# An mLSTM cell with expert routing: output gates as exp(-o) inside the divisor of the output

## The chip, the cores and the metric

The kernel runs on one core of one Trainium2 chip. The metric is device time in microseconds (us) for one execution, and the median of several runs is given. One core has TensorE (PE, matrix multiplication, with PEld for its weight loads), VectorE (DVE), ScalarE (ACT), GpSimd (POOL) and SyncE (SP), which here only issues DMA transfers. The engines run side by side and wait for each other through semaphores.

## The reference

Two parts follow each other. The first is a recurrence over 768 time steps for 4 batches and 8 heads of dimension 40:

```python
for t in range(S):
    m_new = np.maximum(f_gate[:, :, t] + m, i_gate[:, :, t])
    f_stab = np.exp(f_gate[:, :, t] + m - m_new)
    i_stab = np.exp(i_gate[:, :, t] - m_new)
    m = m_new
    C = f_stab[..., None, None] * C + i_stab[..., None, None] * einsum('bhd,bhe->bhde', vt, kt)
    n = f_stab[..., None] * n + i_stab[..., None] * kt
    h_tilde = einsum('bhde,bhe->bhd', C, qt)
    nq = einsum('bhd,bhd->bh', n, qt)[:, :, None]
    denom = np.maximum(np.abs(nq), 1.0)
    o = 1.0 / (1.0 + np.exp(-o_gate[:, :, t]))
    y[:, :, t] = o * h_tilde / denom
```

The result, as 3072 rows of 320 numbers, goes to one of eight experts for each row: `relu(x @ w1[e]) @ w2[e]`, with the expert chosen by a hash of the token. Only the last two lines of the loop matter for the change: the output is `h_tilde` times a sigmoid, divided by `denom`.

## The kernel before

The recurrence is done in chunks: 128 time steps of all eight heads of one batch make one **step**, and there are 24 steps (`NT`), 6 (`NB`) for each of 4 batches. A step has attention scores inside the chunk, a state `C` carried from chunk to chunk, and at its end the transposed output `xo` in PSUM, which holds for each head 40 numbers of `h_tilde` and in column `D` the number `nq`. The expert part follows and reads the rows back by gathers.

The output gates `og` are loaded early, in tiles for six steps, and each tile is put through one sigmoid:

```python
groups = [(0, 3)] + [(s, min(s + 6, NT)) for s in range(3, NT, 6)]

def load_o(s):
    for s0, s1 in groups:
        if s == s0:
            tile_o = ld.tile([P, 6, H, D], F32, name="og", bufs=2)
            og[s, "all"] = tile_o[:, : s1 - s0]
            for i in range(s0, s1):
                og[i] = tile_o[:, i - s0]
    nc.sync.dma_start(og[s], rows_of(o_gate, s))

def sigmoid(s):
    o = og[s, "all"]
    nc.scalar.activation(o, o, AF.Sigmoid)                                      # L343
```

The end of a step, and the parts of a step that the working speaks of:

```python
def back(s):                        # xo in PSUM, tag "tr", 4 buffers
    ...
            nc.tensor.transpose(xo[:, hf, i, :], d["hT"][:, hf, i, :], ident[:])    # L424

def finish(s):
    d = st.pop(s)
    hs = d["xo"].rearrange("p f i (x d) -> p f (i x) d", d=DP)
    den = wk.tile([P, 2, PR, 1], F32, name="den")
    nc.vector.tensor_scalar(den[:], hs[:, :, :, D:D1], scalar1=-1.0, scalar2=1.0,
                            op0=ALU.mult, op1=ALU.max)                          # L430
    nc.vector.tensor_tensor(den[:], den[:], hs[:, :, :, D:D1], op=ALU.max)      # L433
    x = wk.tile([P, H, D], F32, name="x")
    xv = x.rearrange("p (j f) d -> p f j d", f=2)
    nc.vector.tensor_tensor(xv, hs[:, :, :, :D], og[s].rearrange(...), op=ALU.mult) # L436
    nc.vector.reciprocal(den[:], den[:])                                        # L439
    eng = nc.vector if s + 1 == NT else nc.gpsimd
    eng.tensor_tensor(xv, xv, den[:].to_broadcast([P, 2, PR, D]), op=ALU.mult)  # L441
    return lambda: nc.sync.dma_start(x_d[s * P : (s + 1) * P, :], ...)          # L442

def pad_q(b, r):                    # writes qp, read by the transposes of turn_q (L288)
    t = qb[b][r] = qps[2 + r % 2]
    nc.vector.tensor_copy(t[:, :, :D], qb[b]["l"][:, :, r * D : (r + 1) * D])   # L280

def entering(s):                    # qs = q times the decay xb, on VectorE (L327)
def state(s):                       # state product on PE (L382); C += it on VectorE (L388)
def weigh(s):                       # w = scores sp times decays w, on VectorE, twice (L359)
```

The order in which one step is written down (each engine keeps this order for its own instructions):

```python
for s in range(NT):
    b, c = s // NB, s % NB
    # ... loads of k, v, q, o and weights
    decayed(s)                      # POOL: C times its decay (L368)
    turn_k(s + 2)                   # PE: transposes of k (L275), ACT copies them
    turn_q(b + 1, ...)              # PE: transposes of q (L288), ACT copies them
    back(s - 1)                     # PE: xo (L424)
    store = finish(s - 1)           # DVE, POOL
    decays(s + 1)                   # PE (L311), ACT: exp (L315)
    if s > 0 and (s, "all") in og:
        sigmoid(s)
    state(s)
    entering(s + 1)                 # PE: xb (L323), DVE: qs
    k_weights(s + 1)                # POOL: kw (L336)
    store()
    scores(s + 1)                   # PE: sp (L351)
    weigh(s + 1)
    pad_q(nb + 1, r)                # for the transpose of q in the next step
    # ... pieces of the routing
    attend(s)                       # PE: ht (L402, L409), ACT: hT (L417)
    if s == 0:
        sigmoid(0)
    # ... more pieces of the routing (tables on PE, L589, from step 13 on)
back(NT - 1)
finish(NT - 1)()
```

In the last steps of the loop some of these calls fall away. q is transposed one batch ahead, so no q is transposed in the last batch (steps 18 to 23). The first step of a batch has no entering state, so steps 5, 11 and 17, which prepare it, have no `entering`. After the loop, TensorE runs a fixed number of matmuls into an unused tile (`spin`, L924) while the first gathers are under way, and then the experts.

Of the kernel before, what the change touches and what calls it, by code (L numbers as in the profile page):

```python
# [8 lines left out]
F32 = mybir.dt.float32  # L9
# [4 lines left out]
AF = mybir.ActivationFunctionType  # L14
ALU = mybir.AluOpType
PSUM = bass.MemoryType.PSUM

P = 128
# [4 lines left out]
def kernel(  # L23
# [24 lines left out]
    nc = tc.nc  # L48
    B, H, S, D = q.shape
# [6 lines left out]
    NT = N // P  # L56
    PR = H // 2
    DP = 64
    D1 = D + 1
# [20 lines left out]
    x_d = nc.dram_tensor("x_rows", (N, Dm), F32, kind="Internal").ap()  # L80
# [24 lines left out]
    def weight_slices(e):  # L105

        W[e], slices = weights(moe_w1[e], moe_w2[e], wpools[e % 3 // 2], w2pools[2 <= e < 6])
        return slices
# [8 lines left out]
    with tc.tile_pool(name="gates", bufs=1) as gp, \  # L117
# [34 lines left out]
        st = {}  # L152
        qb = {}

        def rows_of(t, s):
            b, c = s // NB, s % NB
            return t[b, :, c * P : (c + 1) * P, :].rearrange("h p d -> p h d")

        def load_k(s):
            st[s] = {"k": ks[s % NK], "v": vs[s % NK]}  # L160
            nc.sync.dma_start(ks[s % NK][:, :, :D], rows_of(k, s))

        def load_v(s):
            nc.sync.dma_start(vs[s % NK][:, :, :D], rows_of(v, s))


        groups = [(0, 3)] + [(s, min(s + 6, NT)) for s in range(3, NT, 6)]
        og = {}

        def load_o(s):  # L170
            for s0, s1 in groups:
                if s == s0:
                    tile_o = ld.tile([P, 6, H, D], F32, name="og", bufs=2)
                    og[s, "all"] = tile_o[:, : s1 - s0]
                    for i in range(s0, s1):
                        og[i] = tile_o[:, i - s0]
            nc.sync.dma_start(og[s], rows_of(o_gate, s))

        def load_q(b, part):

            if part == 0:
                qb[b] = {"l": ld.tile([P, H, NB * D], F32, name="ql", bufs=2)}
            hs = slice(part * PR, (part + 1) * PR)
            nc.sync.dma_start(qb[b]["l"][:, hs], q[b, hs].rearrange("h (p r) d -> p h (r d)", r=NB))

        def load_e(b, gs):
            src = ze_d.rearrange("(g b h) i t -> b (h i) g t", g=NC2, h=H)[b]
            nc.scalar.dma_start(
                Ls[b % 2][: 3 * H, :].rearrange("r (g t) -> r g t", t=W2)[:, gs[0] : gs[-1] + 1],
                src[:, gs[0] : gs[-1] + 1],  # L190
            )
# [78 lines left out]
        def turn_k(s):  # L270
            d = st[s]
            d["kT"] = wk.tile([P, PR, P], F32, name="kT")
            tp = ps.tile([P, PR, P], F32, name="tr", tag="tr", bufs=4)
            for j in range(PR):
                nc.tensor.transpose(tp[:, j, :], d["k"][:, 2 * j : 2 * j + 2, :].rearrange("p h d -> p (h d)"), ident[:])  # L275
            nc.scalar.copy(d["kT"][:], tp[:])
# [5 lines left out]
        def turn_q(b, r, cols):  # L282
            if "T" not in qb[b]:
                qb[b]["T"] = wk.tile([P, PR, S], F32, name="qT")
            t = qb[b].pop(r)
            tp = ps.tile([P, PR, P], F32, name="tr", tag="tr", bufs=4)
            for j in range(PR):
                nc.tensor.transpose(tp[:, j, :], t[:, 2 * j : 2 * j + 2, :].rearrange("p h d -> p (h d)"), ident[:])  # L288
            nc.scalar.copy(qb[b]["T"][:, :, cols], tp[:])  # L289


        def load_q0(c):
            t = qb.setdefault(0, {})[c] = qps[c % 2]
            nc.sync.dma_start(t[:, :, :D], rows_of(q, c))

        def turn_q0(c):
            turn_q(0, c, slice(c * P, (c + 1) * P))
# [40 lines left out]
                    kw_T[:, c % 2, c // 2, b * H : (b + 1) * H].unsqueeze(2).to_broadcast([P, H, D]), op=ALU.mult,  # L338
                )

        def sigmoid(s):
            o = og[s, "all"]
            nc.scalar.activation(o, o, AF.Sigmoid)  # L343

        def scores(s):
            d = st[s]
# [14 lines left out]
        def decayed(s):  # L361
            c = s % NB
            if c == 0:
                st["C"] = None
            if c + 1 < NB:
                st["Cn"] = Cs[s % 2]
                if c > 0:
                    nc.gpsimd.tensor_tensor(  # L368
                        st["Cn"][:, :, :D1], st["C"][:, :, :D1], st[s]["dec"][:].to_broadcast([P, PR, D1]), op=ALU.mult,
                    )  # L370
# [48 lines left out]
        def back(s):  # L419
            d = st[s]  # L420
            xo = d["xo"] = ps.tile([P, 2, 2, P], F32, name="xo", tag="tr", bufs=4)
            for hf in range(2):
                for i in range(2):
                    nc.tensor.transpose(xo[:, hf, i, :], d["hT"][:, hf, i, :], ident[:])  # L424

        def finish(s):
            d = st.pop(s)
            hs = d["xo"].rearrange("p f i (x d) -> p f (i x) d", d=DP)
            den = wk.tile([P, 2, PR, 1], F32, name="den")
            nc.vector.tensor_scalar(  # L430
                den[:], hs[:, :, :, D:D1], scalar1=-1.0, scalar2=1.0, op0=ALU.mult, op1=ALU.max,
            )
            nc.vector.tensor_tensor(den[:], den[:], hs[:, :, :, D:D1], op=ALU.max)  # L433
            x = wk.tile([P, H, D], F32, name="x")
            xv = x.rearrange("p (j f) d -> p f j d", f=2)
            nc.vector.tensor_tensor(  # L436
                xv, hs[:, :, :, :D], og[s].rearrange("p (j f) d -> p f j d", f=2), op=ALU.mult,
            )
            nc.vector.reciprocal(den[:], den[:])  # L439
            eng = nc.vector if s + 1 == NT else nc.gpsimd  # L440
            eng.tensor_tensor(xv, xv, den[:].to_broadcast([P, 2, PR, D]), op=ALU.mult)  # L441
            return lambda: nc.sync.dma_start(x_d[s * P : (s + 1) * P, :], x.rearrange("p h d -> p (h d)"))  # L442


        iotas = {}
# [223 lines left out]
        turn_q0(0)  # L669
        load_q0(2)  # L670
        load_o(0)
        load_v(1)
        load_o(1)
# [48 lines left out]
        for s in range(NT):  # L722
            b, c = s // NB, s % NB
            if 0 < s < NT - 3:
                load_k(s + 3)
                if b == 0 and c < 3:
                    load_q0(c + 3)
            if s + 3 < NT:
                load_v(s + 3)
            if c in (2, 4) and b + 2 < B:  # L730
                load_q(b + 2, c // 2 - 1)
            for i in range(2):
                o = s - (s - 3) % 6 + 6 + 2 * ((s - 3) % 6 - 1) + i if s > 2 else 3 + 2 * s + i
                if o < NT and (s < 3 or 1 <= (s - 3) % 6 <= 3):
                    load_o(o)
            if s in (3, 13):
                slices += weight_slices(s // 10)
            if slices:
                slices.pop(0)()
            decayed(s)  # L740
            if s + 2 < NT:
                turn_k(s + 2)
            if b == 0 and c < 4:
                turn_q0(c + 2)
            if b + 1 < B:
                for r in (turns_of if b else first_turns).get(c, ()):
                    turn_q(b + 1, r, slice(r, None, NB))
            if s > 0:
                back(s - 1)
                store = finish(s - 1)  # L750
            if s + 1 < NT:
                decays(s + 1)
            if s == 0:
                load_e(0, [1, 2])
            if c == 3 and b + 1 < B:
                load_e(b + 1, [0, 1, 2])
            if s > 0 and (s, "all") in og:
                sigmoid(s)
            state(s)
            if s + 1 < NT:  # L760
                entering(s + 1)
                if s + 2 < NT:
                    load_a(s + 2, nc.scalar if s == 0 else nc.sync)
                k_weights(s + 1)
            if s > 0:
                store()
            if s + 1 < NT:
                scores(s + 1)
                weigh(s + 1)
            nb = b + (c == NB - 1)  # L770
            if nb + 1 < B and s + 1 < NT:
                for r in (turns_of if nb else first_turns).get((c + 1) % NB, ()):
                    pad_q(nb + 1, r)
            for piece in before.get(s, []):
                piece()
            attend(s)
            if s == 0:
                sigmoid(0)
                gates_turn(g1)
            for piece in after.get(s, []):  # L780
                piece()
        back(NT - 1)
        finish(NT - 1)()

    wpools.append(ctx.enter_context(tc.tile_pool(name="wlate", bufs=1)))
    w2pools.append(ctx.enter_context(tc.tile_pool(name="w2late", bufs=4)))
# [88 lines left out]
    with tc.manual_schedule():  # L875
# [54 lines left out]
        for e in range(E):  # L930
            g, i = e // EG, e % EG
            if e + 2 < E:
                fetch(e + 2)
            h = xp.tile([P, FB, CAP], F32, name="h")
# [23 lines left out]
    with tc.If(nx > 0):  # L958
        with tc.For_i(0, nx, 1) as k:
# [12 lines left out]
            h = xp.tile([P, FB, CAP], F32, name="h")  # L972
# [34 lines left out]
```

## Time and profile before

| What | Value |
|---|---|
| median of 3 runs (lowest to highest) | 426.49 us (426.43 to 426.70) |
| span of the profiled execution | 423.8 us |
| mean granted TensorE clock, share of full speed | 0.988 |
| TensorE busy | 392.1 us, 93% of the span |
| VectorE busy | 136.2 us, 32% |
| ScalarE busy | 134.3 us, 32% |
| GpSimd busy | 117.7 us, 28% |

The profile divides the span into the start of the recurrence (0 to 38 us), its steps (38 to 165 us) and the experts (165 to 424 us). A group row gives the line, the engine, the operation, the tiles and their shapes (partitions x elements), the count, the busy time in us with the mean of one in ns, and after the last bar the idle time of the engine just ahead of these instructions with what ended it. A timeline row gives start and duration in us, the engine, the line and the tiles; in brackets stands the idle time ahead of it and what ended that. Rows that merge several instructions show their count. A busy TensorE isn't TensorE at its peak, because matmuls are pipelined.

### The profile page before, as it was taken

The page shows a single profiled execution, that of the slowest core. Times are in us where ns is not written, and L with a number is a line of the kernel's source. Part 1 is how long each engine was busy: PE and PEld are TensorE (multiplying, and loading weights), DVE is VectorE, ACT ScalarE, POOL GpSimd, SP SyncE. Part 2 cuts the span into 40 slices and gives each one's busy share as a digit, 9 for nine tenths or more (in the row PEclk, how much of TensorE's full clock was granted, in tenths as well). Part 3 has the DMA queues.
Part 4 walks back from the last instruction along what each step waited for, and adds up shares of the span by engine and source line. Part 5 has one row for each costly group of instructions (what it writes and reads, how often), then busy time and mean ns, then how long its engine had stood idle before and what let it go on. Part 6 is the DMA issues. An engine that isn't in the chain of part 4 may idle for free.

```text
span 423.8 us, 7461 instructions
## 1 busy us (share of the span) xinstructions
PE 392.1 (93%) x2892; PEld 262.1 (62%) x2892; DVE 136.2 (32%) x373; ACT 134.3 (32%) x238; POOL 117.7 (28%) x202
## 2 busy tenths in 40 slices
PE   2369999999999997999999999999999999999992
PEld 2247877877887874556657556556556566575551
DVE  7364748776675762220120110210110201201100
ACT  5158786696495471010111111110111101111010
POOL 6364313313433421711402401311302212020021
PEclk9988999999999999999999999999999999999998
DMA  9829998899675630548508217144126100000000
GB/s 173 212 61 177 205 206 188 191 207 223 153 163 126 162 95 33 151 147 254 168 26 263 87 62 224 63 125 160 60 96 185 62 17 29 0 17 30 0 18 30
DMA packets 111784, 51.37 MB, mean 121 GB/s; under 512 B 86624, under 2 KB 105892, under 8 KB 111748
## 3 DMA queue, kind: packets, MB, share of 16 engines
q1 hardware_dynamic: 105898, 39.31, 38.2%
q0 software_dynamic: 2496, 8.20, 6.0%
q10 hardware_dynamic: 3354, 3.37, 2.4%
q8 instruction: 23, 0.38, 0.4%
q14 instruction: 13, 0.11, 0.1%
HBM read 42.00 MB, written 8.63 MB: 119 GB/s over the span
## 4 chain that ended last, share of the span: by engine, by line
PE 84%; ACT 5%; issue 5%; POOL 2%; DVE 1%; ACTq 1%; DMA 1%; POOLq 0%; DVEq 0%
PE mh L836 22%; PE zp L865 21%; PE sp L351 7%; PE ht L409 6%; PE mh L829 6%; PE ht L402 3%; PE mh L924 3%; PE ab L311 2%; PE tr L275 2%; PE xo L424 2%; PE ht L382 2%; PE tr L288 2%; PE tk L589 2%; PE tp L811 1%; PE xb L323 1%
## 5 line engine op out<-in xcount | busy, mean ns | idle before, releaser
L865 PE MATMUL zp<-w2t,h 128*128 128x320 f32 x384 | 105.2, 433 | 0.0
L836 PE MATMUL mh<-xT,w1t 128*128 128x416 f32 x256 | 96.2, 519 | 0.5 <-issue 0.5
L865 PEld LDWEIGHTS zp<-w2t,h 128*128 128x128 f32 x384 | 72.7, 190 | 32.1 <-issue 3.3
L836 PEld LDWEIGHTS mh<-xT,w1t 128*128 128x128 f32 x256 | 46.7, 190 | 42.7 <-issue 41.6
L817 DVE COPY xT<-tp 128x384 f32<-128x384 f32 x16 | 8.9, 558 | 141.4 <-PE tp L813 98.1
L798 POOL DMA_INDIRECT out_dram<-zo,s_idx x26 | 25.7, 988 | 92.5 <-ACT zo L797 92.5
L845 ACT ACTIVATE h<-mh 128x416 f32<-128x416 f32 x32 | 16.6, 517 | 107.4 <-PE mh L829 54.7
L797 ACT COPY zo<-zp 128x320 f32<-128x320 f32 x26 | 11.1, 426 | 101.1 <-PE zp L865 92.9
L843 DVE TENSOR_SCALAR h<-mh 128x416 f32<-128x416 f32 x32 | 18.9, 592 | 52.1 <-PE mh L829 26.3
L359 DVE TENSOR_TENSOR w<-sp,w 128x512 f32<-128x512 f32 x48 | 30.9, 686 | 13.7 <-PE sp L351 10.3
L441 POOL TENSOR_TENSOR x<-x,den 128x320 f32<-128x320 f32 x23 | 16.6, 724 | 61.6 <-DVE den L439 29.6
L351 PE MATMUL sp<-qT,kT 64*128 64x128 f32 x384 | 29.7, 297 | 4.1 <-ACT qT L289 4.1
L351 PEld LDWEIGHTS sp<-qT,kT 64*128 64x128 f32 x384 | 24.9, 199 | 10.7 <-ACT qT L289 5.9
L315 ACT ACTIVATE w<-ab 128x512 f32<-128x512 f32 x48 | 26.8, 614 | 4.6 <-PE ab L311 4.6
L409 PE MATMUL ht<-w,v 128*64 128x128 f32 x384 | 27.1, 285 | 0.0
L791 POOL DMA_INDIRECT xg<-x_rows,g_idx x24 | 23.4, 974 | 12.6 <-issue 12.6
L829 PE MATMUL mh<-xT,w1c 64*128 64x416 f32 x128 | 26.7, 535 | 0.0
L952 POOL COPY hrem<-h 128x256 f32<-128x256 f32 x8 | 3.2, 400 | 81.9 <-ACT h L845 81.9
L417 ACT COPY hT<-ht 128x512 f32<-128x512 f32 x24 | 14.1, 587 | 31.2 <-PE ht L409 31.2
L409 PEld LDWEIGHTS ht<-w,v 128*64 128x64 f32 x384 | 21.2, 140 | 4.0 <-issue 3.1
L289 ACT COPY qT<-tr 128x512 f32<-128x512 f32 x24 | 22.9, 977 | 0.6 <-PE tr L288 0.3
L275 PE MATMUL tr<-ident,k 128*128 128x128 f32 x96 | 17.4, 309 | 4.1 <-POOL R L638 4.1
(181 smaller groups left out, 421.3 us busy)
## 6 DMA issues: line engine op xcount, KB each, us to landing
w2t<-in_moe_w_dram SPq DMA_DIRECT2D x28, 320.0 KB
w1t<-in_moe_w_dram SPq DMA_DIRECT2D x28, 256.0 KB
k<-in_k_dram SPq DMA_DIRECT2D x24, 160.0 KB
v<-in_v_dram SPq DMA_DIRECT2D x24, 160.0 KB
og<-in_o_gate_dram SPq DMA_DIRECT2D x24, 160.0 KB
x_rows<-x SPq DMA_DIRECT2D x24, 160.0 KB
ql<-in_q_dram SPq DMA_DIRECT2D x6, 480.0 KB
w1c<-in_moe_w_dram SPq DMA_DIRECT2D x14, 128.0 KB
```

What stands on the lines that cost most here:

```text
L275: nc.tensor.transpose(tp[:, j, :], d["k"][:, 2 * j : 2 * j + 2, :].rearrange("p h d -> p (h d)"), ident[:])
L289: nc.scalar.copy(qb[b]["T"][:, :, cols], tp[:])
L315: nc.scalar.activation(w[:, hf], ab[:], AF.Exp)
L351: nc.tensor.matmul(sp[hf][:, j, :], lhsT=d["kT"][r, j, :], rhs=q_of(s)[r, j, :], start=True, stop=True,)
L359: nc.vector.tensor_tensor(d["w"][:, hf], d["sp"][hf][:], d["w"][:, hf], op=ALU.mult)
L409: nc.tensor.matmul(place(j, hf), lhsT=d["v"][:, 2 * j + hf, :], rhs=d["w"][:, hf, j, :], start=(c == 0 and j0 == 0), stop=True, skip_group ...
L791: nc.gpsimd.indirect_dma_start(out=xg, out_offset=None, in_=x_d[:, :], in_offset=bass.IndirectOffsetOnAxis(ap=idx, axis=0),)
L798: ins = nc.gpsimd.indirect_dma_start(out=out[:, :], out_offset=bass.IndirectOffsetOnAxis(ap=idx, axis=0), in_=zo[:], in_offset=None, bound ...
L829: nc.tensor.matmul(hp[i][:, :cols], lhsT=w1c[r, fp, :], rhs=xT[r, 2, :cols], start=first, stop=not first,)
L836: nc.tensor.matmul(hp[i][:, :cols], lhsT=w1t[:, db, fb * P : (fb + 1) * P], rhs=xT[:, db, :cols], start=(first and db == 0), stop=(not fir ...
L843: nc.vector.tensor_relu(h[:, 2 * fp, :cols], hp[i][:, :cols])
L865: nc.tensor.matmul(zp[:], lhsT=h[:, fb, j * P : (j + 1) * P], rhs=w[2][:, fb, :], start=(fb == 0), stop=(fb == FB - 1),)
```

## The change

The sigmoid needs exp, an addition and a division, and the output needs a division by `den` anyway. The new kernel forms `den * (1 + exp(-o))` and divides once: o * h / den = h / (den * (1 + exp(-o))). ScalarE then uses exp alone, the function of the decays, so its function table stays the same throughout. Since nothing has to be gathered for the sake of the table, o is loaded and gated one step at a time, three steps ahead, in five small tiles. `1 + exp(-o)` and its product with `den` are made on GpSimd; the reciprocal, now over all 320 numbers of a partition instead of 8, and the product with `h_tilde` are on VectorE. `finish` is split: `divisor` stands where `finish` stood, and the rest moves behind `entering` and `k_weights`, to give GpSimd time for its product.

```diff
-        groups = [(0, 3)] + [(s, min(s + 6, NT)) for s in range(3, NT, 6)]
         og = {}
         def load_o(s):
-            for s0, s1 in groups:
-                if s == s0:
-                    tile_o = ld.tile([P, 6, H, D], F32, name="og", bufs=2)
-                    og[s, "all"] = tile_o[:, : s1 - s0]
-                    for i in range(s0, s1):
-                        og[i] = tile_o[:, i - s0]
-            nc.sync.dma_start(og[s], rows_of(o_gate, s))
+            og[s] = ld.tile([P, H, D], F32, name="og", bufs=5)
+            nc.sync.dma_start(og[s][:], rows_of(o_gate, s))
...
-        def sigmoid(s):
-            o = og[s, "all"]
-            nc.scalar.activation(o, o, AF.Sigmoid)
+        def gate(s):
+            nc.scalar.activation(og[s][:], og[s][:], AF.Exp, scale=-1.0)
+            nc.gpsimd.tensor_scalar(og[s][:], og[s][:], scalar1=1.0, scalar2=None, op0=ALU.add)
...
+        def divisor(s):
+            d = st[s]
+            hs = d["hs"] = d["xo"].rearrange("p f i (x d) -> p f (i x) d", d=DP)
+            den = wk.tile([P, H, 1], F32, name="den")
+            dv = den.rearrange("p (j f) d -> p f j d", f=2)
+            nc.vector.tensor_scalar(
+                dv, hs[:, :, :, D:D1], scalar1=-1.0, scalar2=1.0, op0=ALU.mult, op1=ALU.max,
+            )
+            nc.vector.tensor_tensor(dv, dv, hs[:, :, :, D:D1], op=ALU.max)
+            o = og[s]
+            eng = nc.vector if s + 1 == NT else nc.gpsimd
+            eng.tensor_tensor(o[:], o[:], den[:].to_broadcast([P, H, D]), op=ALU.mult)
+
         def finish(s):
-            ... (den, max, x = xo * og, reciprocal of den, x * 1/den: as above)
+            hs = st.pop(s)["hs"]
+            o = og.pop(s)
+            nc.vector.reciprocal(o[:], o[:])
             x = wk.tile([P, H, D], F32, name="x")
+            ov, xv = (t.rearrange("p (j f) d -> p f j d", f=2) for t in (o, x))
+            nc.vector.tensor_tensor(xv, hs[:, :, :, :D], ov, op=ALU.mult)
+            nc.sync.dma_start(x_d[s * P : (s + 1) * P, :], x.rearrange("p h d -> p (h d)"))
...
-            for i in range(2):
-                o = s - (s - 3) % 6 + 6 + 2 * ((s - 3) % 6 - 1) + i if s > 2 else 3 + 2 * s + i
-                if o < NT and (s < 3 or 1 <= (s - 3) % 6 <= 3):
-                    load_o(o)
...
             if s > 0:
                 back(s - 1)
-                store = finish(s - 1)
+                divisor(s - 1)
             decays(s + 1)
-            if s > 0 and (s, "all") in og:
-                sigmoid(s)
+            gate(s)
             state(s)
             entering(s + 1)
             k_weights(s + 1)
             if s > 0:
-                store()
+                finish(s - 1)
+            if s + 3 < NT:
+                load_o(s + 3)
             scores(s + 1)
             weigh(s + 1)
             ...
             attend(s)
-            if s == 0:
-                sigmoid(0)
         back(NT - 1)
-        finish(NT - 1)()
+        divisor(NT - 1)
+        finish(NT - 1)
```

More of the change, by code (lines that the diff above doesn't have):

```diff
@@ L424, in back @@
                     nc.tensor.transpose(xo[:, hf, i, :], d["hT"][:, hf, i, :], ident[:])
-        def finish(s):
[L427 to L433, printed above, removed]
-            x = wk.tile([P, H, D], F32, name="x")
[L435 to L442, printed above, removed]
+        def divisor(s):
[10 more added lines that the diff above has]
+            eng.tensor_tensor(o[:], o[:], den[:].to_broadcast([P, H, D]), op=ALU.mult)
+        def finish(s):
+            hs = st.pop(s)["hs"]
+            o = og.pop(s)
+            nc.vector.reciprocal(o[:], o[:])
+            x = wk.tile([P, H, D], F32, name="x")
+            ov, xv = (t.rearrange("p (j f) d -> p f j d", f=2) for t in (o, x))
+            nc.vector.tensor_tensor(xv, hs[:, :, :, :D], ov, op=ALU.mult)
+            nc.sync.dma_start(x_d[s * P : (s + 1) * P, :], x.rearrange("p h d -> p (h d)"))
         iotas = {}
```

## The prediction

> **What bounds the kernel now.** I read the busy time by stretch first, then the groups of instructions, then the timeline of one step. The change touches only the recurrence (24 steps, about 38 to 165 us), so that stretch matters, not the whole span:
>
> ```profile
> core 0: us, PE busy (x) PEld busy (x) DVE busy (x) ACT busy (x) POOL busy (x), PEclk, DMA share, GB/s
> 38.00:165.00 127.00, 121.77 (x1750) 97.41 (x1748) 84.23 (x249) 84.62 (x139) 42.52 (x80) 1.00 0.74 168
> ```
>
> TensorE is busy for 121.77 of 127 us. VectorE and ScalarE each have some 42 us free, GpSimd 84. So whatever is taken off ScalarE can give back at most the 5.2 us in which TensorE stands still. What the change takes off ScalarE, from the groups of instructions (busy us, mean ns, then idle before it):
>
> ```profile
> L343 ACT ACTIVATE og<-og 128x1920 f32<-128x1920 f32 (+1 forms) x5 | 7.4, 1486 | 0.1
> L343 ACT ACT_TABLE_LOAD x5 | 6.4, 1283 | 0.1
> L315 ACT ACT_TABLE_LOAD x5 | 6.4, 1283 | 0.1
> ```
>
> Five sigmoids, five loads of their table and five loads back to exp: 20.2 us of ScalarE. And what concerns VectorE, with shapes kept apart:
>
> ```profile
> L436 DVE TENSOR_TENSOR x<-xo,og 128x320 f32<-128x320 f32 x24 | 11.7, 487 | 0.0
> L439 DVE RECIPROCAL den<-den 128x8 f32<-128x8 f32 x24 | 4.6, 193 | 0.0
> L523 DVE TENSOR_TENSOR_SCAN ove<-ovt,zero_e 128x8 f32<-128x8 f32 x1 | 0.2, 175 | 0.0
> L524 DVE TENSOR_TENSOR b<-ove,ovt 128x8 f32<-128x8 f32 x1 | 0.2, 166 | 0.0
> L534 DVE COPY xe_f<-ove 1x1 f32<-1x1 f32 x1 | 0.1, 134 | 0.0
> ```
>
> All of the last four handle at most 8 numbers per partition. The reciprocal is the slowest of them although it has a single input. That is the row on which this prediction turns. Last, one ordinary step in the timeline (start, duration, engine):
>
> ```profile
> 76.22 0.60 PE L288 MATMUL tr<-ident,qp 128*128 128x128 f32 x4
> ...
> 76.65 0.60 PE L424 MATMUL xo<-ident,hT 128*128 128x128 f32 x4
> ...
> 77.29 0.17 DVE L430 TENSOR_SCALAR den<-xo 128x8 f32<-128x8 f32 x1 [1.23 <-PE xo L424]
> ...
> 77.57 0.49 DVE L436 TENSOR_TENSOR x<-xo,og 128x320 f32<-128x320 f32 x1
> ...
> 77.98 0.19 DVE L439 RECIPROCAL den<-den 128x8 f32<-128x8 f32 x1
> ...
> 78.37 0.33 DVE L388 TENSOR_TENSOR C<-C,ht 128x164 f32<-128x164 f32 x1 [0.20 <-PE ht L382]
> ...
> 78.61 0.68 DVE L327 TENSOR_TENSOR qs<-qT,xb 128x512 f32<-128x512 f32 x1
> ...
> 79.72 1.29 DVE L359 TENSOR_TENSOR w<-sp,w 128x512 f32<-128x512 f32 x2 [0.42 <-PE sp L351]
> ...
> 80.92 0.32 DVE L280 COPY qp<-ql 128x320 f32<-128x320 f32 x1
> ...
> 81.66 0.60 PE L288 MATMUL tr<-ident,qp 128*128 128x128 f32 x4
> ```
>
> The transpose of q (L288) at 81.66 needs the padded q, which VectorE writes last in its step, at 80.92 to 81.24. The slack is 81.66 - 81.24 = 0.42 us. VectorE's free time in this step lies before den (1.23), before C (0.20) and before w (0.42), not in one piece.
>
> **What the Trainium skill says.** "ScalarE: Activation LUTs", section "Table sets: the hidden batching unit": exp and sigmoid are the anchors of different sets, so going from one to the other loads a table; the trace agrees, with ten loads of 1283 ns for five sigmoids. "VectorE: DVE Perf Modes", section on the TRN2 errata: an fp32 tensor_tensor of N elements takes (N+151)/0.96 ns; for 320 that is 491, and the trace has 487 to 492. The same page, section "First, the fixed hardware budget": Reciprocal is done by iterative-divide operations "with a repeat count of 8". It states no time for it. No run here shows a wide reciprocal; the 193 ns for 8 elements is the only measurement.
>
> **The change part by part.**
>
> 1. ScalarE. The 20.2 us go. In their place stand 24 Exp of 128x320. The two forms of the sigmoid took 1004 ns for 960 elements and 1805 for 1920, thus 0.83 ns for each and 203 fixed; 320 make 470 ns, times 24 = 11.3 us. Exp is the table already loaded. Net -8.9 us on an engine with 42 us free. By stretches of one step, TensorE's idle time in the steps with a sigmoid is about 0.5 us at step 3, 0.4 at step 9, nothing at step 15 (118 to 124 us, 6.00 of 6.00 busy), part of 0.7 at step 21, and some 0.6 us hangs on the first one, which holds up the kT copy at 36.15. I choose **-2 us** for all.
>
> 2. GpSimd. The multiplication by 1/den becomes one by den, same size (724 ns). Added: +1 on 128x320. Copies of 192 and 256 elements took 345 and 400 ns, so about 0.45 us, 24 times, 11 us on an engine that is two thirds idle. **0 us.**
>
> 3. Loads of o. Same 24 transfers, now three steps ahead, and later in the queue. A step takes over 5 us, so the data are there. **0 us.**
>
> 4. VectorE, per step. Den and max stay (0.33), the product with xo stays (0.49). The 8-element reciprocal (0.19) goes, and one over **128x320** comes: its duration R is the whole question. For its slope I take (193 - fixed)/8. With fixed = 158 (a tensor_tensor of 8 less 8 cycles) it is 4.4 ns; with fixed = 134 (the 1x1 copy, one input as here) it is 7.4; eight cycles of the page's 0.96 GHz would be 8.3. That gives R = 0.16 + 320 x 0.0044 = 1.6, or 0.13 + 320 x 0.0074 = 2.5, or 2.8 us. I choose 6.3 ns, **R = 2.15 us**. If the extra 27 to 59 ns were only a longer pipeline, R would be 0.5.
>
> 5. Where it lands. In the order of VectorE's instructions in the built kernels, the new sequence is den, max, C, qs, reciprocal, product, w, w, qp, where the old one had product and small reciprocal ahead of C. Ahead of C they filled a gap that VectorE spent waiting for TensorE's state product; now they stand between qs and w. TensorE's transpose of q waits for qp, then xo, decays, state and xb follow it in TensorE's order, and these release den, C and qs. So it is a **ring**. From the timeline: qs ends (79.29) 3.07 us after the q transpose starts (76.22); then R, the product (0.45 after overlap), w twice (1.25), qp (0.28) and 0.1 to the next q transpose: 5.15 + R. With R = 2.15 that is 7.3 us against 5.44 (81.66 - 76.22), **+1.86 us** for an ordinary step.
>
> 6. The sum. Steps 2 to 4 transpose q twice and take about 5.9 us; their ring is longer by 0.9: 3 x 2.25 = 6.8. Seven ordinary steps (6 to 10, 12, and half each of 1 and 17): 7 x 1.86 = 13.0. Steps 5 and 11, ahead of a new batch, have no qs: 2 x 0.8 = 1.6. Steps 13 to 16 also build routing tables on TensorE and take 6.0 already: 4 x 1.3 = 5.2. Steps 18 to 22 transpose no q: there VectorE's own work is the limit, about 4.3 + R + small waits = 6.6 against 5.5: 5 x 1.1 = 5.5. Together 32.1.
>
> 7. The end. The first spin of the expert phase (L924) starts at 165.14, released by VectorE's last work on xo, and the gathers wait for the last x. The den product (0.5, on VectorE in this step, as before) and R now stand ahead of the product with xo: +0.5 + R - 0.1 = 2.5 us. The last but one reciprocal also holds up the last den by about 0.7. **+3.2 us**, fully visible, because the number of spins is fixed. The expert phase itself (250 of 259 us TensorE) is untouched.
>
> Sum: -2 + 32 + 3 = +33, less about 2 because a slower recurrence leaves its other small idle times hidden: **426.5 + 31 = 457 us**.
>
> **The rivals.**
> - *The reciprocal streams one element per cycle.* Then R = 0.5, the ring is 5.65 against 5.44, some 3 us for all steps, +1.5 at the end, -2 from ScalarE: about 429, the same within 2%. For it: 27 ns more than a tensor_tensor could be latency. Against it: a scan over 8 elements costs 175, and the scans over 256 and 512 (679 and 1267 ns) show 2.3 ns each, which explains its excess over 166 in full; the reciprocal's larger excess fits a larger slope in the same way.
> - *The table loads were the real limit*, and the gain is the 8.9 us of ScalarE: 418 or so. Against it: TensorE had only 5.2 us idle in the whole recurrence, and the sigmoid of step 15 cost none.
> - *VectorE has room.* 42 us free against 24 x (2.15 - 0.19) = 47 added: it would just not fit, so some +10 us, 437. I think the ring counts for more than the total, since the free time lies where VectorE waits for TensorE.
> - *GpSimd's product is late* and holds the reciprocal. It starts after max and takes 0.72 while C and qs take about 1.0 plus waits, so it should be hidden: nothing.
>
> **Range and chances.** A step's change follows R with a factor near 1 over some 21 steps and the end: 446 for R = 1.6, 457 for 2.15, 471 for 2.8. The range 439 to 474 holds these; it leaves out the streaming rival, to which I give 0.12. Faster by over 2% would need 8.5 us out of 5.2 us of idle time: 0.03.
>
> **What the profile after will show.** No table load but the first; 24 Exp near 470 ns; a 128x320 reciprocal near 2.15 us (1.6 to 2.8), or 0.5 if I am wrong; steps of 7.3 us with TensorE waiting for the padded q ahead of its transpose; VectorE near 130 us busy in the recurrence, that stretch longer by some 30 us; the expert phase unchanged from its first spin on. The prediction fails most simply if R is 0.5; it fails in size if the ring is relieved, for instance because w and qp aren't the work TensorE waits for.

## Result and profile after

The changed kernel takes **460.08 us** (459.69 to 460.16, four runs); the kernel before took 426.6 in the same session. The ratio is 1.078, 95% interval 1.0761 to 1.0799: 33 us slower, where 457 was predicted.

The busy time by stretch, over the recurrence as it now lies:

```profile
core 0: us, PE busy (x) PEld busy (x) DVE busy (x) ACT busy (x) POOL busy (x), PEclk, DMA share, GB/s
38.00:198.05 160.05, 127.10 (x1746) 99.03 (x1742) 130.98 (x251) 76.08 (x146) 65.38 (x103) 0.97 0.60 134
```

The stretch is 160 us instead of 127. TensorE's work is nearly the same (127.10 us against 121.77), but it now stands still for 33 us. VectorE has gone from 84.23 to 130.98. The groups of instructions (busy us, mean ns, then idle before) show why, and that the table loads are gone but for the first:

```profile
L436 DVE RECIPROCAL og<-og 128x320 f32<-128x320 f32 x24 | 51.5, 2147 | 3.8 <-POOL og L431 3.6
L335 ACT ACTIVATE og<-og 128x320 f32<-128x320 f32 x24 | 11.3, 472 | 0.0
L630 ACT ACT_TABLE_LOAD x1 | 1.3, 1283 | 4.7 <-DMA k<-in_k_dram 4.7
L336 POOL TENSOR_SCALAR og<-og 128x320 f32<-128x320 f32 x24 | 24.2, 1009 | 14.8 <-ACT og L335 12.2
```

One wide reciprocal takes 2.15 us. The timeline of one ordinary step shows where it stands:

```profile
87.95 0.63 PE L281 MATMUL tr<-ident,qp 128*128 128x128 f32 x4 [1.67 <-DVE qp L273]
...
89.06 0.17 DVE L425 TENSOR_SCALAR den<-xo 128x8 f32<-128x8 f32 x1 [0.98 <-PE xo L417]
...
90.14 0.33 DVE L381 TENSOR_TENSOR C<-C,ht 128x164 f32<-128x164 f32 x1 [0.72 <-PE ht L375]
90.38 0.68 DVE L320 TENSOR_TENSOR qs<-qT,xb 128x512 f32<-128x512 f32 x1
90.98 2.15 DVE L436 RECIPROCAL og<-og 128x320 f32<-128x320 f32 x1
93.16 0.49 DVE L439 TENSOR_TENSOR x<-xo,og 128x320 f32<-128x320 f32 x1
93.56 1.28 DVE L352 TENSOR_TENSOR w<-sp,w 128x512 f32<-128x512 f32 x2
94.76 0.32 DVE L273 COPY qp<-ql 128x320 f32<-128x320 f32 x1
95.22 0.63 PE L281 MATMUL tr<-ident,qp 128*128 128x128 f32 x4 [1.69 <-DVE qp L273]
```

From one transpose of q (L281) to the next are 7.27 us. VectorE runs without a gap from C to qp, TensorE waits 1.67 to 1.69 us for qp ahead of its transpose, and then VectorE waits 0.98 and 0.72 us for TensorE: the two engines alternate. Each holds the other up by part of the step although neither is busy throughout.

Where the 34.6 us of the profiled span (458.4 against 423.8) lie, by the starts of `den` and of the first spin in both traces: from the first `den` to the last 158.02 us against 128.0 (**+30.0**); from the last `den` to the first spin 3.81 against 0.91 (**+2.9**); from there to the first expert matmul 14.3 against 12.6 (**+1.7**); the rest of the experts 246.0 in both.

### The profile page after: what moved, and what is told of

It reads as the page before. It is cut to its first block, busy times and chain, and to the rows that moved or that the text cites. A ratio compares the mean times of both kernels' runs of the same rounds, so it can differ in the third digit from the quotient of the medians.

```text
span 458.4 us, 7510 instructions
## 1 busy us (share of the span) xinstructions
PE 399.8 (87%) x2892; PEld 265.1 (58%) x2892; DVE 182.6 (40%) x373; ACT 125.1 (27%) x247; POOL 141.4 (31%) x226
## 4 chain that ended last, share of the span: by engine, by line
PE 69%; DVE 17%; issue 6%; POOL 2%; DMA 2%; ACT 2%; ACTq 0%; POOLq 0%; DVEq 0%
PE mh L831 20%; PE zp L860 20%; DVE og L436 7%; DVE w L352 6%; PE mh L824 6%; PE sp L344 3%; PE ht L402 3%; PE tr L281 3%; PE mh L919 3%; PE ab L304 2%; PE xo L417 2%; PE ht L375 2%; PE tr L268 1%; PE tp L806 1%; PE ht L395 1%
## 5 line engine op out<-in xcount | busy, mean ns | idle before, releaser
L860 PEld LDWEIGHTS zp<-w2t,h 128*128 128x128 f32 x384 | 72.7, 190 | 32.1 <-issue 3.3
L436 DVE RECIPROCAL og<-og 128x320 f32<-128x320 f32 x24 | 51.5, 2147 | 3.8 <-POOL og L431 3.6
L281 PE MATMUL tr<-ident,qp 128*128 128x128 f32 x96 | 16.8, 308 | 23.8 <-DVE qp L273 19.8
L431 POOL TENSOR_TENSOR og<-og,den 128x320 f32<-128x320 f32 x23 | 16.6, 722 | 52.2 <-DVE den L428 52.2
L336 POOL TENSOR_SCALAR og<-og 128x320 f32<-128x320 f32 x24 | 24.2, 1009 | 14.8 <-ACT og L335 12.2
L281 PEld LDWEIGHTS tr<-ident,qp 128*128 128x128 f32 x96 | 12.1, 158 | 27.5 <-ACT kT L269 19.1
## 6 DMA issues: line engine op xcount, KB each, us to landing
w1c<-in_moe_w_dram SPq DMA_DIRECT2D x14, 128.0 KB
```

The source lines that it names most:

```text
L336: nc.gpsimd.tensor_scalar(og[s][:], og[s][:], scalar1=1.0, scalar2=None, op0=ALU.add)
L436: nc.vector.reciprocal(o[:], o[:])
L860: nc.tensor.matmul(zp[:], lhsT=h[:, fb, j * P : (j + 1) * P], rhs=w[2][:, fb, :], start=(fb == 0), stop=(fb == FB - 1),)
```

## Experiments

Each was run beside the kernel before, and its ratio is to that. The ratio is estimated from the runs, with its 95% interval in brackets, and can differ by up to 0.3% from the quotient of the two medians. "Leaves out" says what part of the computation an experiment doesn't do.

### The reciprocal over 8 of the 320 numbers

Leaves out nearly all of the division; everything else of the change stays.

```diff
-            nc.vector.reciprocal(o[:], o[:])
+            nc.vector.reciprocal(o[:, :, 0:1], o[:, :, 0:1])
```

> The changed kernel with its reciprocal over 8 of the 320 numbers of a partition instead of all (the division by the rest is left out). Everything else of the change stays: Exp each step, +1 and product on GpSimd, single loads, the late place of the product. If the width of the reciprocal is the whole cost, the ring of a step falls from 7.27 to 7.27 - 2.15 + 0.19 = 5.3 us, below what TensorE needs, and the time is that of before less the gain on ScalarE, plus some 0.5 us at the end: 424 to 427 us. If the new order, the single loads or GpSimd (its +1 takes 1009 ns) cost something of their own, it stays above 432.

Measured: 427.91 against 427.81, ratio 0.9991 (0.9971 to 1.0012). Its group of reciprocals:

```profile
L436 DVE RECIPROCAL og<-og 128x8 f32<-128x8 f32 x24 | 4.8, 201 | 3.7 <-POOL og L431 3.6
```

All else of the change (Exp, +1, loads one step at a time, the new order) remains in this kernel and costs nothing; nor does it gain anything measurable. The whole loss hangs on the width of this one instruction.

### The reciprocal over half of them

Leaves out half of the division.

```diff
+            nc.vector.reciprocal(o[:, : H // 2, :], o[:, : H // 2, :])
```

> The changed kernel with the reciprocal over 160 of the 320 numbers (half of the division left out). If VectorE's reciprocal has a constant cost for each number, it takes about 0.13 + 160 x 0.0063 = 1.14 us, and an ordinary step 6.27 us where TensorE needs 5.44 (6.0 with routing tables). The time should then fall by about 1.0 us for some 15 steps and the end, with a smaller part for steps that TensorE limits already: 440 to 446 us. If the cost lies in the pipeline and not in the number of elements, the time stays near 460.

Measured: 436.15 us, ratio 1.0176 (1.0131 to 1.0221).

```profile
L436 DVE RECIPROCAL og<-og 128x160 f32<-128x160 f32 x24 | 27.5, 1148 | 3.7 <-POOL og L431 3.6
```

The duration is a straight line: (2147 - 1148)/160 and (1148 - 201)/152 both give 6.2 ns for each number per partition, with some 0.15 us fixed. The ordinary step became 6.27 us, so 1.0 us of reciprocal is 1.0 us of step (7.27 - 6.27). The total fell below the expected range because the steps that build routing tables lost the same full 1.0 us, where a smaller part had been expected of them, and because four long steps of the changed kernel lost 1.75 to 1.86 us each; a low clock had added to these, as is shown further down. The steps with routing tables, at 6.1 us before and 6.28 here, nearly hide a reciprocal of half the width.

### The +1 left out

Leaves out the addition of 1 on GpSimd, to test the rival that GpSimd is late.

```diff
-            nc.gpsimd.tensor_scalar(og[s][:], og[s][:], scalar1=1.0, scalar2=None, op0=ALU.add)
```

> The changed kernel without the addition of 1 on GpSimd (left out; the output is then h / (den * exp(-o))). GpSimd loses 24 x 1.01 us. If GpSimd isn't on the path, the time stays within 1 us of 460. If its work (the late product with den, or kw behind the addition) holds up VectorE or TensorE, the time falls by 3 us or more.

Measured: 461.42 us, ratio 1.0772 (1.0728 to 1.0817), as with it. GpSimd's 24 us of additions are off the path. The other half of that rival, GpSimd's product with `den`, shows in four places of the trace after, all where no `qs` stands between `den` and the reciprocal, for instance:

```profile
67.66 2.15 DVE L436 RECIPROCAL og<-og 128x320 f32<-128x320 f32 x1 [0.90 <-POOL og L431]
```

VectorE waits 0.90 us for it each time, 3.6 us in all, with and without the +1. The kernel with the narrow reciprocal has the same four waits and is no slower than the kernel before; whether they cost something beside the wide one was not tested by a run.

### Reciprocal and product behind what TensorE waits for

Nothing is left out. `finish(s - 1)`, and the load of `o` behind it, move after the two products w and the padded q.

```diff
-            if s > 0:
-                finish(s - 1)
-            if s + 3 < NT:
-                load_o(s + 3)
             if s + 1 < NT:
                 scores(s + 1)
                 weigh(s + 1)
             ... (pad_q)
+            if s > 0:
+                finish(s - 1)
+            if s + 3 < NT:
+                load_o(s + 3)
```

> The changed kernel with reciprocal and product moved behind the scores' weighting (w, w) and the padding of q (qp) in VectorE's order; the same work, nothing left out. If the ring through qp is what counts, TensorE's transpose of q no longer waits for the reciprocal; the next ring goes through the PSUM buffer of xo, which the decays of the next step take over: 1.2 us to C, 0.9 to the end of qs, 1.3 for w, 0.3 for qp, 2.2, 0.5 and 0.1 = 6.4 us for an ordinary step instead of 7.27, some 13 us less in all: 445 to 450 us. If VectorE's total work is what counts, nothing changes: 458 to 462 us.

Measured: 461.17 us, ratio 1.0754 (1.0702 to 1.0806): no gain, a clear miss. The waits in the recurrence (engine, line, what it waited for: us, times, longest):

```profile
PE ab L304 <- DMA R<-decay_pieces: 9.6, 10, 2.4
PE tr L268 <- DMA k<-in_k_dram: 8.8, 7, 1.9
PEld L304 <- DMA R<-decay_pieces: 8.7, 12, 1.5
```

TensorE no longer waits for the padded q but for loads. In the program's order, SyncE issues the store of x ahead of the next step's loads. It waits for the product with xo, which had become late, and the loads stand behind it in SyncE's order. One wait had taken the place of the other, and between 109 and 134 us the granted clock was low as well (0.69 to 0.94), so this kernel alone says nothing about the ring.

### The same, with the store of x put off

Nothing is left out. As above, but each store of x is issued one step later, behind the loads of the coming step, and the load of `o` is back where the change has it.

```diff
-            nc.sync.dma_start(x_d[s * P : (s + 1) * P, :], ...)
+            stores.append(lambda: nc.sync.dma_start(x_d[s * P : (s + 1) * P, :], ...))
...
                     load_a(s + 2, nc.scalar if s == 0 else nc.sync)
                 k_weights(s + 1)
+            if s > 1:
+                stores.pop(0)()
```

> As the run with reciprocal and product behind qp, but with the store of x put off by a step, behind the loads of the decay pieces in SyncE's order; nothing left out. In that run TensorE no longer waited for qp but for transfers (decay pieces and k), which stood in SyncE's queue behind the store that waits for the late product. If this queue closed the ring there, its waits go, VectorE's own work of some 5.5 us and the routing pieces sets the step, about 6.2 us, and the time falls to 436 to 446 us. If VectorE's total alone already set the 461 us, it stays above 455.

Measured: 447.69 against 428.35, ratio 1.0471 (1.0418 to 1.0523), somewhat above the expected range. The waits for loads are gone: those for R, 9.6 and 8.7 us above, are 0.3 and 0.2. Busy time by stretch (columns as in the first fence), two ordinary steps and then a step with routing tables:

```profile
90.00:103.00 13.00, 11.88 (x172) 9.02 (x170) 12.72 (x25) 7.46 (x14) 4.61 (x7) 1.00 0.83 198
131.00:138.00 7.00, 6.37 (x91) 5.17 (x91) 6.05 (x13) 3.80 (x8) 2.71 (x4) 1.00 0.61 135
```

So the loss has two parts. By the two ratios, (1.078 - 1.0471) x 426.6 = **13 us** of it come from where the reciprocal stands: they return when TensorE no longer waits for it. (Some 3 of them are the falls of the clock described below, which this kernel's profiled run doesn't have.) The other **20 us** stay. In the profiled run 16.9 of them lie between the first and the last `den` (144.87 us against 128.0) and 2.9 behind it.

VectorE's amount of work explains only a part of these. In six of the middle steps (from `den` to `den` at 70.11 to 82.56 and 89.46 to 113.62 us) it is busy for 35.9 of 36.6 us, so no other order of the same instructions within them can make them shorter; they took 32.4 us before, which makes 4.2 of the 16.9. In the other steps that grew, VectorE has 0.5 to 1.8 us free in each, in those with routing tables for instance (6.05 of 7.0 us); what holds them was not isolated. Over the whole stretch VectorE has 130.1 us of work, only just more than the 128.0 that the stretch took before.

### The kernel before, with Exp in place of Sigmoid

Leaves out the 1 + and the division of the gate; takes the other ten table loads from ScalarE and adds nothing.

```diff
-            nc.scalar.activation(o, o, AF.Sigmoid)
+            nc.scalar.activation(o, o, AF.Exp, scale=-1.0)
```

> The kernel before with Exp of -o in place of the sigmoid in the same five instructions (1 + and the division are left out). It takes away the ten table loads (12.8 us of ScalarE) and nothing else. By the idle time of TensorE in the steps with a sigmoid the gain is about 2 us: 424 to 425.5 us. If the table loads are the limit of these steps, it is up to 9 us: 417 to 420.

Measured: 426.05 against 426.55, ratio 0.9997 (0.9979 to 1.0014). Taking the ten loads off ScalarE gains nothing measurable. At step 11 this kernel was 1.7 us ahead (its `den` at 92.60 us against 94.28), but steps 12 and 13 then took 6.01 and 6.03 us instead of 5.13 and 5.20. In its waits the loads of the decays show up:

```profile
PEld L311 <- DMA R<-decay_pieces: 2.1, 6, 0.9
PE ab L311 <- DMA R<-decay_pieces: 1.8, 2, 1.1
```

Before, the first of these lines reads 0.3 us in 2 waits. The two waits of the second line, 1.09 and 0.68 us, fall in just these two steps. The loads of o, two at a time, stand ahead of those of the decays in SyncE's order, so the likely reading is that the gain ran into them; the next two kernels bear on that, but do not isolate it.

### A gate by tanh, and then one step at a time

Nothing is left out. The gate is (1 + tanh(o/2))/2: tanh in place of the sigmoid, +1 on GpSimd, and the factor 2 in the divisor, at no further instruction. This has the change's aim (no second table) without a wide reciprocal.

```diff
-            nc.scalar.activation(o, o, AF.Sigmoid)
+            nc.scalar.activation(o, o, AF.Tanh, scale=0.5)
+        def plus(s):
+            nc.gpsimd.tensor_scalar(og[s], og[s], scalar1=1.0, scalar2=None, op0=ALU.add)
...
-                ... hs[:, :, :, D:D1], scalar1=-1.0, scalar2=1.0, op0=ALU.mult, op1=ALU.max,
+                ... hs[:, :, :, D:D1], scalar1=-2.0, scalar2=2.0, op0=ALU.mult, op1=ALU.max,
-            nc.vector.tensor_tensor(den[:], den[:], hs[:, :, :, D:D1], op=ALU.max)
+            nc.vector.scalar_tensor_tensor(
+                den[:], in0=hs[:, :, :, D:D1], scalar=2.0, in1=den[:], op0=ALU.mult, op1=ALU.max,
+            )
```

> The kernel before with the sigmoid as (1 + tanh(o / 2)) / 2: tanh on ScalarE in the same five instructions, +1 on GpSimd each step, and the factor 2 folded into den, so that the small reciprocal stays. Nothing is left out. If tanh needs no table load beside exp, it gains what the run with Exp alone gains, 1 to 3 us (423.5 to 425.5). If loads come back with tanh, or GpSimd's additional 1 us each step is in the way, it is at or above the kernel before.

Measured: 426.63 us, ratio 1.0001 (0.9987 to 1.0015). The second kernel also loads and gates o one step at a time, three steps ahead, as the change does:

```diff
-                    tile_o = ld.tile([P, 6, H, D], F32, name="og", bufs=2)
+            og[s] = ld.tile([P, H, D], F32, name="og", bufs=5)
...
+            plus(s)
+            if s + 3 < NT:
+                load_o(s + 3)
```

> As the run with tanh, but with o loaded and gated one step at a time, three steps ahead, as in the change. Nothing is left out. ScalarE has 24 tanh of 0.47 us instead of five long ones of 1.0 to 1.8 us, so no step carries a long one. Expected another 0 to 1.5 us: 422.5 to 425 us. If loading step by step costs something, it is slower than the grouped one by more than 0.5 us.

Measured: **423.3 us** (422.96 to 424.21), ratio 0.9937 (0.9917 to 0.9957). This version beats both kernels, by 0.6% over the one before. Its groups of instructions have a single table load, of 1283 ns, and in its waits that for the decays is as small as before:

```profile
PEld L305 <- DMA R<-decay_pieces: 0.2, 1, 0.2
```

"ScalarE: Activation LUTs" of the Trainium skill, section "Table sets: the hidden batching unit", lists tanh in exp's set; the single load agrees. The other function alone gives 1.0001, with single loads 0.9937; single loads with the sigmoid were not run, so what they give by themselves is not shown.

## Why the prediction was right, and where its terms were off

**Step 4, the reciprocal: right.** 2.15 us was chosen, 2.147 measured. That it came this close has luck in it, since the working allowed 1.6 to 2.8; the three widths then showed a straight line of 6.2 ns, so the argument from 8 numbers (excess over a simple instruction is slope, not latency) holds. The streaming rival is out, and so is the reading of "VectorE: DVE Perf Modes", "First, the fixed hardware budget", as eight clock cycles for each number: by an estimate from the page's 0.96 GHz, 6.2 ns are six cycles. (The trace before has the product of 320 numbers at 483 to 492 ns; the prediction read 487 to 492.)

**Step 5, the ring: right, but not the whole loss.** 7.3 us was predicted and 7.27 measured, with TensorE waiting for qp as foretold: over the recurrence, L281 waits for it 13 times, 19.8 us in all. Against the rival "VectorE has room" the prediction held that the ring counts for more than VectorE's total. With the ring opened 13 of the 33 us return and 20 remain, twice the 10 that the rival's own sum gave. In six steps what is then uncovered is VectorE's total, close behind the ring; in most of the rest it is a limit that no run isolated.

**Step 6, the sum: right in total, off in its terms.** From the first `den` to the last it came to +30.0, against 32.1 less the 2 for ScalarE and the 2 for hidden idle time. Here period n is the time from the `den` before to that of step n, so that it holds mostly the work of step n - 1; of the half steps 1 and 17 in the prediction's sum, the first is counted with the early steps and the second with the last:

| part | predicted, us | measured, us |
|---|---|---|
| steps up to 4 (periods 2 to 5) | +7.7 | +4.7 |
| middle (periods 6 to 17) | +18.0 | +21.7 |
| end (periods 18 to 24) | +6.4 | +3.6 |

The early and the last steps had been given a full share of R. They grew less: periods 2 to 5 came to 7.3 to 7.7 us, where the ring with its 0.9 for the second transpose gives 8.2, and had been 5.8 to 6.8 already; among the last, with no q to transpose, periods 22 and 23 hardly changed (4.97 and 5.32 us before, 5.05 and 5.04 now). The middle ones grew by more, and there most of the cause can be seen. Periods 7, 8, 13 and 14 took 8 us and not 7.27. In the timeline after, the starts of `den`, and the transpose between the first two:

```profile
73.02 0.17 DVE L425 TENSOR_SCALAR den<-xo 128x8 f32<-128x8 f32 x1
...
79.11 0.97 PE L281 MATMUL tr<-ident,qp 128*128 128x128 f32 x4 [2.22 <-DVE qp L273]
...
80.97 0.17 DVE L425 TENSOR_SCALAR den<-xo 128x8 f32<-128x8 f32 x1 [0.97 <-PE xo L417]
...
89.06 0.17 DVE L425 TENSOR_SCALAR den<-xo 128x8 f32<-128x8 f32 x1 [0.98 <-PE xo L417]
```

The four transposes take 0.97 us and not 0.63, because the granted clock was low after the wait of 2.22 us. In the busy time by stretch PEclk is the third value from the right, 0.56:

```profile
79.10:83.00 3.90, 3.89 (x32) 2.86 (x32) 1.26 (x8) 2.50 (x4) 0.72 (x1) 0.56 0.90 169
```

Two periods take 7.95 and 8.09 us. The kernel without the +1 waited just as long there in its profiled run, kept its clock at this place, and gives the same stretch undisturbed:

```profile
72.31 0.17 DVE L424 TENSOR_SCALAR den<-xo 128x8 f32<-128x8 f32 x1
...
78.41 0.63 PE L281 MATMUL tr<-ident,qp 128*128 128x128 f32 x4 [2.22 <-DVE qp L273]
79.51 0.17 DVE L424 TENSOR_SCALAR den<-xo 128x8 f32<-128x8 f32 x1 [0.21 <-PE xo L416]
86.78 0.17 DVE L424 TENSOR_SCALAR den<-xo 128x8 f32<-128x8 f32 x1 [0.98 <-PE xo L416]
```

That is 14.47 us for the two periods instead of 16.04: one fall of the clock costs 1.6 us. The changed kernel had two (the second at step 14, clock 0.62 from 124 to 128 us, another wait of 2.21), thus about 3.2 of the 3.7 us by which the middle term was too small. The prediction had no term for that. (The kernel without the +1 did not escape either: behind its second wait of 2.22 us the clock was 0.50 from 123 to 125 us, and period 14 took 8.19.) Periods 6 and 12, the steps without qs, grew by 1.5 us each where 0.8 was taken. They are among the steps in which the reciprocal waits 0.90 us for GpSimd's product; the prediction held the product to be hidden, by C and qs. The other middle steps grew by 0.8 less in all than predicted.

**Step 7, the end: right** but for one part. From the last `den` to the first spin +2.9 us, where 0.5 + R - 0.1 = 2.5 was worked out; the 0.7 for a late last `den` is not to be seen separately, as it lies inside the +30.0. Not foreseen: the spin itself. Its line after:

```profile
198.09 9.92 PE L919 MATMUL mh<-w1t,ident 128*128 128x416 f32 x22 [5.21 <-DVE x L439]
```

Before, the same 22 matmuls took 7.92 us after a wait of 1.02; here the clock is 0.79 from 198.05 to 208. "Fully visible, because the number of spins is fixed" held for the number, not for their pace, and the expert phase was not unchanged from its first spin on: it took 1.7 us more. The length of the spin is not settled by the wait alone: the version with Exp waited 1.02 us and took 9.6.

**Step 1, ScalarE: wrong in size.** -2 us was taken for the absent table loads, and both tests show nothing: 0.9991 with the rest of the change and 0.9997 without it. An early lead of 1.7 us did exist and was lost again at steps 12 and 13. In the version with tanh and single loads the stretch from the first `den` to the last is 1.9 us shorter than before (126.1 against 128.0), so a gain of the size of this term was to be had, but not in the changed kernel; how much of it the table loads are was not isolated.

**Step 2, GpSimd: the term was mis-sized, without effect.** 1009 ns was measured for one +1 where 0.45 us was estimated from copies, and leaving it out changes nothing. What shows of GpSimd is its product, in the steps without qs. **Step 3, the loads: 0**, as predicted, and in the version with tanh the single loads even belong to what gains.

The total of 457 against 460.08 thus rests on two terms that were right (R, the ordinary ring) and on others that cancel: early and last steps 5.8 too high, the middle 3.7 too low, the 4 taken off for ScalarE and hidden idle time not to be had, the first spin's 1.7 missing.

## What to carry to other kernels

Before an instruction is made wider, measure what it takes per number, not what it takes now: the narrow reciprocal looked as cheap as any other, and its width alone cost 33 us. To be rid of a second activation table, look for a function in the table that is already there (here tanh for the sigmoid) rather than one that needs a division over the full tile. And when work is moved later in an engine's order, look at the DMA queue that waits for its result: a store behind a late product held up the loads behind it, and the gain of 13 us showed only once the store was moved too.

## What the hardware showed unexpectedly

- VectorE's reciprocal of fp32 took 201, 1148 and 2147 ns for 8, 160 and 320 numbers: 6.2 ns each, where the product of 320 takes 490.
- GpSimd took 1009 ns for adding a constant to 128x320 and 722 for multiplying a tile of that size by 8 numbers per partition that are spread over it; the instruction with one input tile is the slower one.
- Of the four waits of 2.2 us on TensorE in the changed kernel and the one without the +1, three were followed by some 4 us at a low granted clock (0.56 and 0.62 in the first kernel, down to 0.50 in the second), which cost 0.9 to 1.6 us in this ring. One passed without it, and the waits of 1.7 us in the ordinary steps never brought it.
